# Value products of groups 16 to 19 in fp32 instead of six bf16 products each, with a new instruction order

## The chip, the cores and the metric

The kernel runs on one core of a Trainium2 chip. Its time is the device time of one execution in microseconds (us). The core has a matrix engine (TensorE, "PE" in the profile, with its weight loads as "PEld"), VectorE ("DVE"), ScalarE ("ACT"), GpSimd ("POOL"), and SyncE ("SP"), which here only issues the DMA transfers. Each engine works through its own queue in order.

## The reference, cut to what matters

Three layers follow one another. The first is a gated linear attention over 4 batches, 8 heads, 768 steps and 40 dimensions a head, the second a feed-forward layer that takes the largest of three products, and the third a feed-forward layer with a clipped activation.

```
for t in range(S):                       # S = 768, state C is 40x40 a head
    m_new  = max(f[t] + m, i[t])
    f_stab = exp(f[t] + m - m_new);  i_stab = exp(i[t] - m_new)
    C = f_stab*C + i_stab * outer(v[t], k[t])
    n = f_stab*n + i_stab * k[t]
    y[t] = sigmoid(o[t]) * (C @ q[t]) / max(abs(n . q[t]), 1)
x = y as 3072 tokens x 320
h = max(x @ w1, x @ w2, x @ w3)          # 320 -> 768
x = h @ w_out                            # 768 -> 320
h = x @ w_in                             # 320 -> 2048
out = (h * clip(h + 3, 0, 6) / 6) @ w_out2
```

## The kernel before, in words

The 768 steps are cut into six chunks of 128. A group `g` is one chunk of one batch with its 8 heads, so there are 24 groups; chunk `c` holds groups 4c to 4c+3. Within a group the recurrence becomes matrix products: `sc` (line 585) makes the scores of keys against queries, DVE multiplies them by the decay factors into the tile `fd` (line 601), and `pv` (line 663) multiplies that 128x128 tile of each head with the gated values `vt` (128 rows, 42 columns: 40 values and two for the denominator). `inter` adds what the state of the chunk before gives, `dc` makes the new state, `tr` transposes the finished group into `x1`.

The value product exists in two forms. For a group below `G3` it is one fp32 matmul a head. For the others, `vt` and `fd` are each split into three bf16 parts (functions `vr0`, `vr1` for the values and `pr0`, `pr1`, in two halves, for the scores: lines 648, 651, 657 and 661, six instructions a group on DVE or POOL), and the product is made of the six bf16 matmuls a head that `PARTS` lists:

```
pp = top(s["fd"]), top(s["pr"]), low(s["pr"])
vv = top(s["vt"]), top(s["vr"]), low(s["vr"])
for h in range(H):
    for n, (a, r) in enumerate(PARTS):
        nc.tensor.matmul(ps[:, h], pp[a][:, h], vv[r][:, h], start=n == 0, stop=n == len(PARTS) - 1)
```

The first feed-forward layer (`f_in`, line 325 for its products, and `f_out`, lines 913 and 915) runs on blocks of two or four groups as these get ready, in between the attention's matmuls. A first block needs groups 0 and 1. The second layer (`quad`, products at line 1251, output at line 1372) comes last, in 48 steps of a block of four groups and a pair of hidden slices. Its weights arrive as 64-bit numbers and are turned into two fp32r tiles each by ACT, DVE and POOL (`convert`, `pair_prep`, `o_prep`); the rows that are shared by four pairs are copied into each weight tile by DMA (`mix`, line 1138, three transfers a tile, 32 such copies in all).

Nothing decides the order at run time. `Plan` numbers all operations with what they depend on, the list `ORDER` says in which sequence they are issued (each engine takes its own operations out of that one list), the set `POOLS` says which of the operations that either may do go to POOL instead of DVE, and `JUNK` puts idle bf16 matmuls on a tile of ones (128x512, line 1444) ahead of some PE operations near the start, which fill gaps of PE there and give nothing to the result.

Of the kernel before, what the change touches and what calls it, by code (L numbers as in the profile page):

```python
# [29 lines left out]
NBC, GF, G3 = 4, 8, 16  # L30
# [10 lines left out]
1 990 2 4 5 6 991 992 7 8 993 10 11 9 13 14 994 900 20 918 902 901 19 995 12 40 903 904 919 15 18 16 23 905 920 50 22 21 921 922 17  # L41
24 42 906 907 923 39 912 28 908 914 62 930 913 44 41 43 25 27 63 45 26 909 46 910 47 911 29 915 916 105 924 64 917 48 49 51 960 65
30 31 67 66 931 37 84 932 936 32 33 61 926 925 52 106 53 54 942 927 68 34 38 72 3 35 36 55 59 108 107 111 81 82 94 928 60 56 933 86
69 57 58 85 89 929 110 71 70 109 112 128 948 934 1044 935 113 73 937 1045 938 943 944 939 74 1046 940 125 126 116 83 114 945 127
1048 75 88 941 950 122 1047 87 1052 117 946 947 129 115 1049 949 123 118 119 124 954 972 955 130 956 76 951 952 139 120 3290 1053
121 77 90 953 1054 996 957 140 141 1056 91 958 962 961 959 1055 1060 966 968 963 78 1050 93 92 964 967 965 103 95 133 151 969 984 79
1061 183 974 970 978 131 1057 80 973 1051 971 975 96 976 132 1062 1064 977 1063 97 104 135 979 980 981 1002 134 150 162 224 160 982
986 161 1008 98 99 1068 985 1065 137 136 983 138 164 100 101 998 1058 987 163 988 142 102 1059 1026 997 989 152 143 1069 153 999 144
1003 1000 1004 155 165 1001 1070 194 171 1066 166 172 1072 256 1076 1077 1067 1014 1071 167 1010 1009 1005 173 1073 182 1006 170
1011 145 146 1078 1012 1079 168 169 1007 1015 174 192 1016 196 1013 184 1080 1082 1017 195 1018 1086 1087 1020 1081 1083 203 193  # L50
1074 1021 1022 154 1023 1019 197 204 258 156 215 1088 1090 1027 1084 205 198 175 1085 226 176 1028 199 1024 1029 1025 225 1038 1075
1032 177 1089 1030 260 1091 1033 1034 200 1092 214 1096 1093 229 178 1097 1098 185 201 216 1031 228 235 206 236 237 157 202 1035 186
1039 1100 227 231 158 1036 1037 1099 1040 207 1041 1094 1042 1102 1101 1106 296 259 208 1103 147 1107 297 247 159 266 261 336 262
230 233 1104 1108 1110 232 263 264 234 218 268 1105 246 298 299 248 1109 300 257 265 238 1111 1095 188 338 301 148 267 1112 1113
1116 269 1117 1114 303 1118 1119 149 1120 304 187 239 376 1043 302 1122 1121 1123 1115 340 179 240 241 242 217 1126 1127 1128 1130
1134 1135 339 1129 219 270 272 287 306 271 189 1131 309 341 1136 1124 342 305 274 273 1138 220 1125 180 190 181 1141 1143 243 1137
307 276 277 1139 1142 327 343 1145 278 209 210 1149 1150 378 191 344 244 346 221 211 315 1132 245 1144 1146 222 1133 286 212 213 308
288 1151 1152 1153 1155 1159 316 275 279 1154 223 310 312 311 250 252 1160 1161 379 381 290 345 280 281 313 1156 1147 1148 1162 289
456 458 337 314 348 367 1163 1164 282 349 326 1165 318 380 317 1169 1170 352 1166 319 292 249 251 347 383 384 1171 1173 1157 253
1158 416 382 291 293 1172 350 354 459 418 1175 461 377 460 419 389 421 1179 1174 254 1176 283 1180 320 294 386 321 420 366 423 388  # L60
328 1167 1168 255 284 355 322 387 368 527 390 295 285 1181 1183 1182 1184 1185 1189 351 385 353 1190 356 323 1177 422 417 1186 357
1178 1140 1191 358 370 369 359 329 463 426 1193 1192 1194 464 392 1195 1196 396 1199 1200 1206 360 361 427 397 1204 536 424 462 1203
1187 1188 1208 1201 1207 428 394 391 1209 1202 538 539 496 362 371 1210 1214 331 393 425 398 1215 465 395 498 330 332 333 334 500
1197 466 335 399 1211 1198 499 406 429 324 325 1216 1217 501 540 431 432 407 400 497 1218 401 430 408 433 372 373 374 402 403 446
503 434 404 468 405 504 447 448 1219 1220 435 457 622 502 1224 1225 363 467 438 469 470 487 1212 364 365 471 436 541 1205 437 439
1213 1226 1227 473 509 440 472 486 506 1221 441 1228 442 375 488 1229 474 508 410 1230 1234 1235 576 443 409 444 412 476 515 507 475
510 1236 543 505 1231 544 542 578 1222 477 445 411 1223 413 1238 478 512 479 526 490 1237 1239 514 579 528 613 414 577 580 1240 624
1244 589 625 627 626 629 516 517 598 1245 511 1246 513 518 415 546 1232 581 1233 1241 547 548 545 583 519 449 489 586 584 582 1247
450 628 1248 1250 452 520 521 522 451 529 556 557 1249 1251 1254 1255 453 587 1242 1256 1258 1243 537 454 455 549 492 668 588 1257
1259 480 481 550 551 482 590 552 553 567 1260 1264 1265 670 1268 1252 630 585 714 491 493 554 566 523 558 555 530 568 1261 1253 559  # L70
560 671 1269 596 1271 1273 1266 1272 597 524 716 1267 599 494 717 673 672 675 719 1274 1275 591 593 1276 612 1279 525 592 632 631
1280 595 600 601 634 623 676 718 561 562 1262 1281 1283 563 1263 532 594 760 1282 1284 721 531 674 602 603 1285 533 483 1289 564
1270 565 604 495 1290 762 763 484 1286 669 681 690 614 485 1277 1278 570 572 722 569 605 642 638 1291 571 643 678 764 635 1292 1293
679 633 659 534 680 573 682 1294 636 1295 1299 1300 644 574 640 606 1287 641 677 535 765 683 685 1288 645 692 1296 767 1301 795 797
607 648 658 1302 1303 684 751 686 704 575 1304 694 660 1305 616 618 798 637 639 646 647 649 693 1306 1309 1310 1297 715 768 799 766
705 608 1311 695 688 1313 650 1298 727 1312 1314 720 723 1315 651 1319 1316 1320 1321 691 800 802 1307 652 653 1308 830 724 726 725
1322 1323 696 706 654 729 662 1324 728 687 832 615 769 689 833 617 1325 731 697 733 619 730 655 1326 732 620 770 698 750 761 699 700
1329 1330 796 1317 771 1318 801 778 734 740 1334 1331 736 1336 1337 1333 735 1332 1338 1340 1344 1345 752 1339 656 657 773 738 741
739 1341 737 661 663 772 1327 865 803 621 742 743 1328 701 744 834 781 664 707 804 782 609 702 1346 774 665 1347 1348 666 776 835
867 610 775 783 745 746 805 869 784 703 1350 836 777 785 786 837 831 838 667 1349 1354 747 1355 748 611 787 807 749 810 1351 1356  # L80
1342 1343 1357 812 806 1358 868 808 870 872 1360 1499 1500 840 813 708 1501 816 1502 814 1359 820 821 871 1503 1364 1365 779 1507
1352 1361 1353 815 841 843 809 811 780 1366 1368 788 1367 842 1505 1508 709 1504 1506 1370 1374 1375 789 866 1369 873 839 1376 818
1362 754 1363 819 817 1335 1510 1377 1371 874 1520 851 852 1512 1513 1521 1522 790 844 822 791 878 1378 710 711 1380 1384 1379 1385
1381 712 875 1372 1514 823 846 1373 886 877 845 792 1386 1387 1388 847 855 876 853 824 825 1390 1394 854 1515 756 753 713 755 757
758 856 880 879 1389 1395 881 1391 848 1401 888 1396 793 1382 882 1511 1523 1509 1524 1516 1527 1528 1397 1383 887 890 889 891 1402
1398 759 1525 1526 1403 857 849 850 858 826 1405 1399 892 884 859 1409 1529 1530 1404 1517 1518 860 861 885 1410 862 794 883 893 894
827 1519 895 896 1411 1531 1532 1406 1534 1536 1537 897 1547 828 1392 1393 1413 1573 863 1412 1533 829 898 864 1575 1414 1838 899
1415 1419 1574 1576 1577 1535 1544 1420 1421 1545 1546 1839 1407 1416 1408 1549 1840 1844 1538 1422 1550 1851 1539 1540 1551 1841
1842 1541 1423 1424 1425 1429 1430 1426 1553 1417 1552 1555 1554 1431 1418 1542 1585 1543 1843 1557 1847 1432 1556 1560 1570 1571
1433 1435 1434 1561 1567 1845 1586 1587 1558 1439 1436 1578 1579 1857 1588 1562 1580 1854 1581 1589 1582 1440 1609 1441 1563 1846  # L90
1427 1428 1591 1590 1611 1855 1592 1443 1583 1442 1610 1584 1848 1615 1616 1621 1860 1612 1444 1625 1593 1617 1445 1594 1596 1568
# [84 lines left out]
JUNK = {20: 17, 19: 5, 15: 2, 42: 1, 41: 2, 63: 6, 47: 1, 64: 4, 51: 3, 37: 1, 34: 1, 59: 1, 81: 2, 86: 1, 69: 1, 85: 2, 1044: 1, 116: 1, 139: 1, 120: 1, 95: 1, 1064: 1, 135: 2, 1070: 1, 171: 3}  # L176
# [1328 lines left out]
```

## Time and profile before

| | |
|---|---|
| median of 3 runs | 734.71 us (731.77 to 736.48) |
| profiled execution, its own time | 733.25 us |
| its span, first to last instruction | 731.5 us |
| PE busy in it | 721.8 us |
| DVE, ACT, POOL busy | 538.3, 386.1, 339.7 us |
| granted TensorE clock | 1.00 |

The span is what the hardware profiler recorded of the profiled execution; its time has 1.75 us more around it. Busy time is the time in which an engine had at least one instruction in work. Matmuls overlap each other, so that the duration of one is longer than the step from one start to the next; what a group of matmuls costs is read from the chain of work, where each piece has the time that it held up the next.

### The profile page before, as it was taken

The numbers are of one execution on the slowest core, as the hardware profiler recorded it, in microseconds if no ns is written. First come the engines' busy times: TensorE is split into PE (matmuls) and PEld (weight loads), VectorE is DVE, ScalarE is ACT, GpSimd is POOL, SyncE is SP. The second block draws the span as 40 slices with busy tenths as digits, with TensorE's granted clock in tenths as the row PEclk, the third lists the DMA queues.
The fourth block names the chain that finished last, engine by engine and source line by source line (L and its number), as shares of the span: only waits on it lengthen the run. The fifth ranks groups of instructions, "written<-read, shape, count | busy, mean of one in ns | idle before, by whom it ended". The sixth has DMA issues, their size and how long they took to land.

```text
span 731.5 us, 15227 instructions
## 1 busy us (share of the span) xinstructions
PE 721.8 (99%) x5685; PEld 654.9 (90%) x5685; DVE 538.3 (74%) x989; ACT 386.1 (53%) x867; POOL 339.7 (46%) x361
## 2 busy tenths in 40 slices
PE   9999999999999999999999999999999999999997
PEld 5789998888887788888888999999999999999997
DVE  6999987686877789687888788576566666567453
ACT  5776644234343244234777776545555555655543
POOL 3547664244345876773445372343433253443320
PEclk9999999999999999999999999999999999999999
DMA  8768675686676665724655521102100300300101
GB/s 268 250 210 291 194 240 187 191 239 212 199 228 198 191 202 180 227 76 143 217 181 178 162 79 59 37 1 59 37 2 1 95 1 1 95 1 1 37 2 37
DMA packets 57418, 95.22 MB, mean 130 GB/s; under 512 B 8096, under 2 KB 31872, under 8 KB 57344
## 3 DMA queue, kind: packets, MB, share of 16 engines
q1 hardware_dynamic: 57344, 94.24, 41.8%
q8 instruction: 45, 0.74, 0.4%
q14 instruction: 29, 0.24, 0.1%
HBM read 74.84 MB, written 17.65 MB: 126 GB/s over the span
## 4 chain that ended last, share of the span: by engine, by line
PE 89%; DVE 4%; DMA 3%; ACT 1%; issue 1%; POOL 1%; SPq 1%; ACTq 0%; DVEq 0%; POOLq 0%
PE h L325 25%; PE po L1372 22%; PE T L1251 12%; PE Q L1251 9%; PE acc L913 6%; PE pv L667 3%; PE sc L593 2%; PE acc L915 2%; PE pv L673 1%; PE dc L752 1%; DMA raw<-in_w 1%; PE tr L722 1%; PE in L625 1%; PE sc L597 1%; DMA kvo<-in_kvo 1%
## 5 line engine op out<-in xcount | busy, mean ns | idle before, releaser
L325 PE MATMUL h<-x,w 128*128 128x512 f32 (+1 forms) x1008 | 217.0, 366 | 0.0
L325 PEld LDWEIGHTS h<-x,w 128*128 128x128 f32 x1008 | 168.3, 189 | 27.8 <-ACT m L879 0.3
L1372 PE MATMUL po<-wo,gg 128*128 128x320 f32 x1152 | 192.5, 310 | 0.4 <-DVE gg L1328 0.4
L1372 PEld LDWEIGHTS po<-wo,gg 128*128 128x128 f32 x1152 | 172.3, 189 | 0.6 <-DVE gg L1328 0.6
L1328 POOL TENSOR_TENSOR gg<-cc,gg 128x512 fp32r<-128x512 f32 x48 | 63.2, 1319 | 141.2 <-ACT gg L1324 121.7
L1297 DVE TENSOR_TENSOR cc<-Q,s 128x512 f32<-128x512 f32 x96 | 53.1, 553 | 53.3 <-ACT s L1283 29.0
L1312 DVE SCALAR_TENSOR_TENSOR cc<-cc 128x512 f32<-128x512 f32 (+1 forms) x96 | 62.4, 654 | 36.0 <-ACT cc L1308 35.8
L1283 ACT COPY s<-T 128x256 f32<-128x256 f32 x144 | 52.8, 367 | 67.7 <-PE T L1251 50.8
L1324 ACT CAST gg<-cc 128x512 fp32r<-128x512 f32 x96 | 58.7, 621 | 33.9 <-DVE cc L1312 27.8
L1308 ACT ACTIVATE cc<-cc,b 128x512 f32<-128x512 f32 (+1 forms) x96 | 59.0, 617 | 27.4 <-DVE cc L1297 27.4
L913 PE MATMUL acc<-hh,w 128*128 128x512 f32 (+1 forms) x246 | 71.6, 370 | 0.0
L881 DVE TENSOR_TENSOR m<-h,m 128x512 f32<-128x512 f32 (+1 forms) x82 | 50.1, 611 | 20.4 <-PE h L325 17.8
L894 ACT CAST hh<-m 128x512 fp32r<-128x512 f32 (+1 forms) x41 | 23.0, 562 | 61.9 <-PE acc L913 60.8
L561 DVE TENSOR_TENSOR_SCAN fd<-fd,ident 128x512 f32<-128x512 f32 x40 | 52.3, 1315 | 2.5 <-DMA fd<-f_d 2.3
L913 PEld LDWEIGHTS acc<-hh,w 128*128 128x128 f32 x246 | 43.7, 188 | 6.9
L1328 DVE TENSOR_TENSOR gg<-cc,gg 128x512 fp32r<-128x512 f32 x48 | 36.7, 765 | 14.0 <-ACT gg L1324 13.9
L879 ACT COPY m<-h 128x512 f32<-128x512 f32 (+1 forms) x41 | 21.7, 528 | 42.3 <-PE h L325 31.3
L898 POOL TENSOR_TENSOR hh<-m,hh 128x512 fp32r<-128x512 f32 (+1 forms) x19 | 24.0, 1268 | 27.2 <-ACT hh L894 21.4
L601 DVE TENSOR_TENSOR fd<-sc,fd 128x512 f32<-128x512 f32 x48 | 32.0, 681 | 4.8 <-PE sc L593 2.5
L667 PEld LDWEIGHTS pv<-vt,fd 128*128 128x128 f32 x256 | 30.4, 192 | 0.8
L667 PE MATMUL pv<-vt,fd 128*128 128x42 f32 x256 | 30.4, 280 | 0.0
L915 PE MATMUL acc<-hh,w 128*128 128x512 f32 (+1 forms) x82 | 29.3, 364 | 0.0
(338 smaller groups left out, 1410.9 us busy)
## 6 DMA issues: line engine op xcount, KB each, us to landing
kvo<-in_kvo SPq DMA_DIRECT2D x22, 488.0 KB
fd<-f_d SPq DMA_DIRECT2D x20, 512.0 KB
qs_d<-q SPq DMA_DIRECT2D x48, 160.0 KB
raw<-in_w SPq DMA_DIRECT2D x18, 384.0 KB
qs<-qs_d SPq DMA_DIRECT2D x80, 80.0 KB
qraw<-in_qkf SPq DMA_DIRECT2D x16, 320.0 KB
qs<-qs_d SPq DMA_DIRECT2D x32, 160.0 KB
rawo<-in_w2o SPq DMA_DIRECT2D x16, 320.0 KB
```

What stands on the lines that cost most here:

```text
L325: nc.tensor.matmul(ps, wt[:, a:a + 128], x[:, r], start=n == 0, stop=n == len(order) - 1)
L561: nc.vector.tensor_tensor_scan(out=half, data0=s.get(("bc", a), half), data1=ident4.rearrange("p h t -> p (h t)"), initial=0.0, op0=ALU.mu ...
L667: nc.tensor.matmul(ps[:, h], s["fd"][:, h], s["vt"][:, h], start=True, stop=True)
L913: nc.tensor.matmul(acc[a], wo[:, a * 128:128 + a * 128], h, start=first, stop=last)
L1251: nc.tensor.matmul(ps, w[0:rows, a], x[0:rows, b], start=start and n == 0, stop=n == 3, skip_group_check=not start)
L1283: nc.scalar.copy(s["s", two][:, i % 2], s["T"])
L1297: nc.vector.tensor_tensor(out=x, in0=y, in1=s["s", i == 0], op=ALU.add)
L1308: nc.scalar.activation(s["r"][:, a:b], src, AF.Relu, bias=b3)
L1312: nc.vector.scalar_tensor_tensor(out=s["cc"][:, a:b], in0=s["r"][:, a:b], scalar=6.0, in1=src, op0=ALU.min, op1=ALU.mult)
L1324: nc.scalar.copy(GG[j, p][:, 0, a:b], s["cc"][:, a:b])
L1328: eng.tensor_tensor(out=g[:, 1, a:b], in0=s["cc"][:, a:b], in1=g[:, 0, a:b].bitcast(F32), op=ALU.subtract)
L1372: nc.tensor.matmul(po[j, t], x, WO[2 * p + e][:, o:o + OC], start=first and z == 0, stop=last and z == 2)
```

## The change: four groups' value products and a new order

`G3` goes from 16 to 20. So groups 16 to 19 take the fp32 form of `pv`, and their 24 splitting instructions are gone. As the operations are numbered anew, `ORDER`, `POOLS` and `JUNK` are all replaced.

```diff
-NBC, GF, G3 = 4, 8, 16
+NBC, GF, G3 = 4, 8, 20
...
-JUNK = {20: 17, 19: 5, 15: 2, 42: 1, 41: 2, 63: 6, 47: 1, 64: 4, 51: 3, 37: 1, 34: 1, 59: 1, 81: 2, 86: 1, 69: 1, 85: 2, 1044: 1, 116: 1, 139: 1, 120: 1, 95: 1, 1064: 1, 135: 2, 1070: 1, 171: 3}
+JUNK = {20: 16, 19: 1, 15: 4, 41: 4, 63: 3, 29: 3, 51: 4, 37: 1, 34: 2, 56: 2, 120: 2, 116: 2, 122: 1, 114: 1, 1028: 1, 139: 1, 1038: 1, 150: 1, 100: 3, 171: 2}
```

The lists `ORDER` and `POOLS` are too long to show (3291 numbers before, 3267 after). Taking one engine's operations out of each list and matching them by what they write gives this:

| read from the two lists | before | after |
|---|---|---|
| PE, ACT, SP operations | 881, 847, 288 | 881, 847, 288 |
| DVE, POOL operations | 930, 340 | 934, 312 |
| operations of free choice that change engine | | 130 POOL to DVE, 119 DVE to POOL |
| idle matmuls ahead of the first product of layer one | 51 | 40 |
| idle matmuls behind it | 11 | 15 |
| DVE: place of the scan over gates of chunks 1 to 5 (line 370) | 26th, between `y` of group 0 and the reciprocals of group 1 | 18th, ahead of the scores of group 1 |
| SP: place of the load of those gates | 13th | 8th, ahead of the weights (0,1), (0,2) and (1,1), the q and k of group 1, and the k, v and o of group 2 |
| `mix` copies with at most one PE operation between issue and reader | 5 of 32 | 0 of 32 |
| `mix` copies with at most five | 9 of 32 | 1 of 32 |

The sequence of PE's operations is nearly the same in both: the `pv` of groups 16 to 19 stand at places 214, 236, 242 and 256 before and at 207, 226, 238 and 253 after, and the transposes that end the attention at 310 and 309 or 310.

## Rows read from the trace of the kernel before

**Rows 1.** Head of the page: busy us (share of the span) and instructions.
```profile
PE 721.8 (99%) x5685; PEld 654.9 (90%) x5685; DVE 538.3 (74%) x989; ACT 386.1 (53%) x867; POOL 339.7 (46%) x361
```

**Rows 2.** Busy time by stretch of the span; columns as its second line says.
```profile
core 0: us, PE busy (x) PEld busy (x) DVE busy (x) ACT busy (x) POOL busy (x), PEclk, DMA share, GB/s
0.00:30.64 30.64, 28.85 (x220) 18.05 (x221) 24.37 (x49) 19.23 (x40) 14.86 (x26) 1.00 0.83 252
30.64:221.00 190.36, 189.97 (x1655) 166.53 (x1655) 157.11 (x297) 90.71 (x206) 92.64 (x105) 1.00 0.72 223
221.00:333.00 112.00, 111.62 (x1058) 91.10 (x1057) 89.14 (x149) 38.23 (x83) 79.80 (x82) 1.00 0.57 173
...
381.00:421.00 40.00, 37.57 (x245) 34.54 (x244) 32.30 (x63) 30.23 (x78) 19.24 (x25) 1.00 0.55 167
```

**Rows 3.** All waits of PE, eight lines: us in total, times, longest.
```profile
PE wps L1444 <- DVE gm L366: 1.5, 1, 1.5
PE T L1251 <- DMA w_4d<-mix_d1d: 1.2, 1, 1.2
PE T L1251 <- ACT s L1283: 1.2, 1, 1.2
...
PE tr L722 <- DVE x L733: 0.2, 1, 0.2
```

**Rows 4.** Chain of work, one group's value product: start us, us, what.
```profile
76.62 1.91 PE pv L667 x16
...
207.57 1.72 PE pv L667 x16
226.23 1.22 PE pv L673 x48
...
305.95 1.20 PE pv L673 x48
```

**Rows 5.** Weight loads of the two forms (lines 667, 673): ns min/median/max.
```profile
L667 PEld LDWEIGHTS pv<-vt,fd x256: 186/192/201, 16.9 to 209.0; 128*128 128x128 f32 x128
...
L673 PEld LDWEIGHTS <-fd x192: 96/97/103, 226.1 to 330.0; 128*128 128x128 bf16 x192
```

**Rows 6.** Sum over all stretches for the split tiles, `pr` and `vr`.
```profile
sum 731.60, PE 10.28 PEld 9.42 DVE 5.70 POOL 31.36; mean PE 1.71 PEld 1.57 DVE 0.95 POOL 5.23
...
sum 731.60, PE 10.49 DVE 4.31 POOL 8.36; mean PE 1.75 DVE 0.72 POOL 1.39
```

**Rows 7.** Chain of work up to the first product of layer one.
```profile
7.32 8.10 DMA raw<-in_w
...
16.48 1.24 issue
...
22.47 0.15 DVE gm L369
...
22.64 1.54 DVE gm L370
...
26.97 0.22 PE wps L1444
...
30.64 0.48 PE h L325 x4
```

**Rows 8.** Idle matmuls (line 1444) ahead of and behind that product.
```profile
0.00:30.64 30.64, 16.07 (x51) 4.99 (x51) 1.00 0.83 252
30.64:221.00 190.36, 3.77 (x11) 0.99 (x11) 1.00 0.72 223
```

**Rows 9.** Issues on SP's queue: the raw weights (0,1) and the second gates.
```profile
5.15 0.36 SPq L284 DMA_DIRECT2D raw<-in_w  x1
...
10.84 0.33 SPq L361 DMA_DIRECT2D gf<-in_fg  x1
12.00 0.33 SPq L362 DMA_DIRECT2D gi<-in_ig  x1
```

**Rows 10.** Chain of work where the second layer begins: transfers and SP's queue.
```profile
383.75 3.08 DMA rawo<-in_w2o
387.40 2.88 DMA raw<-in_w2m
...
414.31 2.20 SPq L1138
417.95 1.41 DMA w_4d<-mix_d1d
```

258 rows, old and new, of tables (ORDER, POOLS) are left out of this document.

## The prediction

> **What bounds the kernel now.** I began with the head of the page: PE is busy for 721.8 of 731.5 us [rows 1]. A busy matrix engine could still be one that stretches its work, so I went on to the table by stretch. From the first product of layer one at 30.64 us until 381 us PE is idle for well under a microsecond in a hundred, and the clock is 1.00 throughout [rows 2]. DVE comes next, at 157 of 190 us and then 89 of 112; it is close, but it isn't the bound. Third, PE's own list of waits. It has eight lines. Leave out the 1.5 us at the very start, and the other seven, from 1.2 down to 0.2, add up to 4.4 us [rows 3]; 2.4 of them lie between 381 and 421 us, where the second layer begins (40.00 less 37.57) [rows 2]. So behind 30.64 us the time is the sum of PE's work plus 4.4 us. Ahead of it the chain does not run on PE: it is a weight transfer of 8.10 us, then DVE, and PE fills the time with idle matmuls [rows 7, 8]. This gives the rule for every edit: work added to PE behind 30.64 us costs its full length, work taken off DVE or POOL is worth at most the waits that it ends, and ahead of 30.64 us only the DMA and DVE chain counts.
>
> **The value products.** In the chain of work the 16 matmul records of a group in fp32 hold 1.72 us, once 1.91, and the 48 records of a group in bf16 hold 1.22 or 1.20 [rows 4]. They are fewer, but each step is longer: 1.72 / 16 = 108 ns against 1.22 / 48 = 25 ns. The weight loads show why the fp32 form does not profit from its smaller count: one takes 192 ns against 97 [rows 5], and with 42 columns behind each load the products are too short to cover it. Per group the change costs PE 1.72 - 1.22 = 0.50 us, for four groups +2.0 us, all of it on the path. The far end is the dearest fp32 row against the cheapest bf16 row, 1.91 - 1.20 = 0.71, which makes 2.8. I take 2.0, since 1.7 is what stands beside full-length matmuls as here.
>
> Here a rule speaks the other way. The Trainium skill, "FP8 and Floating Point Precision", section "TensorE Precision Notes", says that a true fp32 product takes four passes through the array. With bf16 passes of 25 ns that would be, as an estimate from this page, 8 x 4 = 32 passes or 0.8 us a group, 0.4 less than the 48 of bf16, and the sum would hold -1.7 instead of +2.0. The fp32 groups of this trace contradict it at this shape, with 1.72 us measured; it is kept below as a rival with a small chance.
>
> **The splitting work that goes.** Over all eight split groups `pr` holds DVE for 5.70 and POOL for 31.36 us, `vr` 4.31 and 8.36 [rows 6]. Half of that, 24 instructions, is 24.9 us, some 20 of it on POOL. None of it lies on the chain while PE is full, so directly it is worth 0. What it can be worth indirectly is limited by the 4.4 us of PE waits, of which hardly any falls where these groups run (0.38 us of idle time in 221 to 333 us). I enter 0. The cover is PE's own backlog; if PE were not full there, DVE's share would come onto the path.
>
> **The start.** In the old order DVE's scan over the later gates, with the small copy ahead of it 1.54 + 0.15 us, stands on the chain between group 0's output and group 1's reciprocals, and group 1 is the last thing that the first block waits for [rows 7]. The new order puts it eight places earlier, near the point where the chain shows 1.24 us in which DVE has nothing released [rows 7]. So about 1.5 us of it leaves the chain. Late next is the weight transfer. The load of these gates also moves, on SP's queue, from 10.84 us to about where the raw weights (0,1) were issued at 5.15 [rows 9], ahead of three weight transfers, q and k of group 1 and the load of group 2. It is 2 x 32 x 640 x 4 bytes = 164 KB, 0.6 us at the 252 GB/s of this stretch [rows 2], and it delays all five. The scan also gets a new place to wait: if its gates are late, the scores of group 1 queue behind it on DVE, and PE's `pv` of group 1 behind those. The start therefore gains between 11 x 0.22 = 2.4 us (the eleven idle matmuls fewer, each 0.22 on the chain [rows 7]) and loses up to 0.6. I take -1.5, the row of the scan itself.
>
> **Idle matmuls behind the start.** There are 15 now; the old order had 11 [rows 8]. PE is full there, so four more cost 4 x 0.22 = +0.9 us, or nothing if they stand where PE waits anyway.
>
> **Where the second layer begins.** Two of PE's waits of 1.2 us are here, one of them for a `mix` copy into a weight tile [rows 3], which was held up 2.20 us in SP's queue before its transfer of 1.41 [rows 10]. The new list issues these copies with a longer lead: only one of 32, instead of nine, has five PE operations or fewer ahead of its reader. I count that wait as gone, -1.2. What is late next is the conversion chain (raw transfers of 3.08 and 2.88 us [rows 10], then ACT, DVE, POOL), which I leave as it is. The ends: -2.4 if all idle time in the stretch goes, and +7.1 if the cover of the chain is lost (below).
>
> **Engines swapped.** 130 operations go from POOL to DVE and 119 the other way; DVE gets four operations more in all, POOL 28 fewer. With DVE at 83% [rows 2] this is nearly balanced, and I enter 0. It is the term that I know least: it can open a wait of a microsecond or two anywhere.
>
> **Sum.** 733.25 + 2.0 + 0.9 - 1.5 - 1.2 = 733.4 us, against the profiled execution. That execution was 1.5 us below the median of the three runs (734.71), so on the scale of the median I forecast 734.9 us: no change that can be seen.
>
> **The rivals.**
> - *Slower: the start of the second layer loses its cover.* Between 381 and 421 us four links of transfer and queue, 3.08 + 2.88 + 2.20 + 1.41 = 9.6 us, lie on the chain, while PE loses only 2.4 us [rows 2, 10]; ACT, DVE and PE are all above 75% there. If the new order brings the first weight tiles late, PE, which takes its products in order, pays the remaining 7.1 us: 734.9 + 1.2 + 7.1 = 743.2 us. It begins to decide once these tiles are more than about 7 us later against PE's work than now. For it: conversions there move by several us both ways in the lists. Against: the copies, which caused the largest wait, get more lead.
> - *Faster: the relief closes the waits.* With 25 us less splitting work all 4.4 us of PE's waits go and the start gains its full 2.4: 733.25 + 2.0 + 0.9 - 4.4 - 2.4 = 729.4, or 730.8 against the median. For it: DVE at 83%. Against: the waits lie elsewhere than the relief. Even this is within 1%, because PE has no more idle time to give.
> - *The fp32 products are cheap.* If a group cost PE 0.4 us less instead of 0.5 more, the sum is 3.7 us lower, 731.2. Against: sixteen groups in this trace at 1.7 to 1.9 us [rows 4].
>
> **How the numbers follow.** The forecast gets 0.75, the slower rival 0.08, the relief 0.11, cheap fp32 products 0.03, and 0.03 stays for a gain that no row shows. One per cent, 7.3 us, is about what a measurement can tell from no change. Forecast, relief and cheap products all lie within it, so "within 1%" has 0.75 + 0.11 + 0.03 less 0.02 for a relief that also shortens PE's work, 0.87; faster has 0.05, slower 0.08. The range goes from 729.5, the relief less a microsecond for the spread of the runs, to 741.0: the dear ends of products (+0.8) and start (+2.1), the wait not ended (+1.2), and 2 us for a new wait.
>
> **What would show it.** In the profile after: 320 fp32 records of `pv` and 192 bf16 ones, with 1.7 us for each of the four new groups in the chain. First product of layer one at about 29 us, without the long scan ahead of it. No PE wait for a `mix` copy. PE idle for 3 to 4 us behind the start. I am wrong if PE's waits between 381 and 421 us grow past 6 us, if DVE passes 95% in a stretch and PE waits for it, or if the fp32 groups take under 1.2 us.

## The result, and the profile after

| | before | after |
|---|---|---|
| median of 7 runs each, one chip | 733.28 us (731.77 to 736.48) | 743.19 us (738.86 to 751.96) |
| ratio, 95% interval | | 1.0125 [1.0093, 1.0157] |
| profiled execution | 733.25 us | 751.96 us |
| its span, mean granted clock | 731.5 us, 1.00 | 750.2 us, 0.984 |

The kernel is slower by 1.25%, some 9 us, and outside the forecast range. The profiled execution of after is the slowest of its seven, 1.8% above the fastest of them, and is one of two that the ratio leaves out. In after the names stand two lines higher than in before: `pv` at 665 and 671, `h` at 323, the idle matmuls at 1442.

The head of the page, with the granted clock in 40 slices, answers to [rows 1]:

```profile
PE 736.2 (98%) x5550; PEld 665.5 (89%) x5550; DVE 538.4 (72%) x994; ACT 384.4 (51%) x867; POOL 308.1 (41%) x335
...
PEclk9589999999999999999999999999999999999999
```

PE is busy 14.4 us longer although it has 135 instructions fewer, and the second and third slice of the clock row read 5 and 8. POOL lost 31.6 us of work, more than the some 20 of the splitting, and the time did not follow it. The same stretches as [rows 2], with the same columns:

```profile
0.00:30.64 30.64, 27.49 (x131) 17.84 (x133) 17.42 (x34) 12.62 (x26) 11.24 (x21) 0.79 0.76 224
30.64:221.00 190.36, 186.35 (x1615) 161.91 (x1611) 155.36 (x288) 89.43 (x205) 89.06 (x100) 0.97 0.68 209
221.00:333.00 112.00, 110.88 (x849) 91.15 (x848) 82.38 (x149) 38.77 (x82) 47.39 (x53) 1.00 0.64 188
381.00:421.00 40.00, 40.00 (x205) 33.96 (x204) 30.12 (x63) 31.39 (x82) 20.03 (x28) 1.00 0.59 172
```

Two places are worse. From 30.64 to 221 us PE is idle for 4.0 us (0.39 before), and the mean clock of the first two stretches is 0.79 and 0.97. One is better: at 381 to 421 us, where PE had lost 2.4 us, it loses nothing. (The same microseconds are not the same work there: the last product of layer one starts at 403.7 us, before at 383.6. But from 381 to 441 us PE has no idle time either.) Cut at the points where the clock changes, the start reads so:

```profile
0.00:17.76 17.76, 14.61 (x73) 7.42 (x75) 12.24 (x25) 9.13 (x18) 6.82 (x15) 1.00 0.89 248
17.76:34.83 17.07, 17.07 (x111) 13.65 (x108) 7.56 (x16) 5.92 (x14) 6.12 (x8) 0.50 0.52 167
34.83:45.07 10.24, 9.07 (x78) 7.26 (x76) 9.95 (x17) 7.82 (x17) 4.85 (x6) 1.00 0.64 179
45.07:51.89 6.82, 6.82 (x35) 5.28 (x31) 4.35 (x11) 4.58 (x15) 3.53 (x6) 0.50 0.69 212
```

TensorE ran at half clock, 1.2 instead of 2.4 GHz, for 17.07 + 6.82 us; half of that, 11.9 us, is what it cost, as an estimate. PE's idle time grew from 9.7 to 14.0 us (span less busy), and four products at the price forecast are 2.0 us: 11.9 + 4.3 + 2.0 = 18.2 of the 18.7 us between the two spans. PE's own list of waits (us in total, times, longest) answers to [rows 3]:

```profile
PE dc L750 <- issue: 2.4, 1, 2.4
PE wps L1442 <- DVE gm L364: 1.5, 1, 1.5
PE h L323 <- ACT m L877: 1.3, 2, 1.1
PE sc L595 <- DMA qs<-in_qk: 1.2, 2, 0.8
PE tr L720 <- POOL y L711: 0.8, 1, 0.8
```

The mix copy is gone from it. In its place stand a state product `dc`, hidden-layer products `h`, and the scores `sc` of group 1; the list of before has no wait above 0.4 us ahead of the second layer but the 1.5 us at the very start.

The chain of work at the start (start us, us, what) shows the last of these; the three `pv` rows at its end answer to [rows 4]:

```profile
3.10 5.35 DMA qs<-in_qk
8.46 8.81 DMA qs<-in_qk
17.41 1.74 PE sc L595 x14
19.15 1.40 PE wps L1442 x3
20.55 3.27 PE pv L665 x16
...
37.67 1.12 DVE t L303
...
272.27 1.91 PE pv L665 x16
289.09 1.80 PE pv L665 x16
306.70 1.22 PE pv L671 x48
```

The scores of group 1 are released by the transfer of its q and k, which took 8.81 us of the chain; right behind, the clock is half and a value product takes 3.27 us. The queue of SP shows that it was issued later; the last line is that transfer in the kernel before:

```profile
4.77 0.42 SPq L359 DMA_DIRECT2D gf<-in_fg  x1
5.24 0.42 SPq L360 DMA_DIRECT2D gi<-in_ig  x1
6.53 0.35 SPq L282 DMA_DIRECT2D raw<-in_w  x1
8.05 0.79 SPq L471 DMA_DIRECT2D qs<-in_qk  x2
```
```profile
5.55 1.18 SPq L473 DMA_DIRECT2D qs<-in_qk  x2
```

With the gates loaded first, the raw weights follow at 6.53 us (5.15 before [rows 9]) and the q and k of group 1 at 8.05, 2.5 us later than before. The first product of layer one starts at 37.75 us, not at the 29 that was forecast.

### The profile page after: what moved, and what is told of

Its sections match the earlier page's. It is cut to its first block, busy times and chain, and to the rows that moved or that the text cites. A ratio compares the mean times of both kernels' runs of the same rounds, so it can differ in the third digit from the quotient of the medians.

```text
span 750.2 us, 14934 instructions
## 1 busy us (share of the span) xinstructions
PE 736.2 (98%) x5550; PEld 665.5 (89%) x5550; DVE 538.4 (72%) x994; ACT 384.4 (51%) x867; POOL 308.1 (41%) x335
## 4 chain that ended last, share of the span: by engine, by line
PE 85%; DVE 6%; DMA 4%; issue 2%; ACT 1%; SPq 1%; POOL 0%; ACTq 0%; DVEq 0%; POOLq 0%
PE h L323 23%; PE po L1370 21%; PE T L1249 12%; PE Q L1249 9%; PE acc L911 6%; PE pv L665 4%; DMA qraw<-in_qkf 2%; DMA qs<-in_qk 2%; PE acc L913 2%; PE sc L591 2%; PE dc L750 2%; PE wps L1442 1%; PE tr L720 1%; PE sc L595 1%; DVE cc L1310 1%
## 5 line engine op out<-in xcount | busy, mean ns | idle before, releaser
L323 PE MATMUL h<-x,w 128*128 128x512 f32 (+1 forms) x1008 | 222.1, 369 | 1.5 <-ACT m L877 1.3
L1326 POOL TENSOR_TENSOR gg<-cc,gg 128x512 fp32r<-128x512 f32 x41 | 53.9, 1318 | 126.6 <-ACT gg L1322 108.4
L1310 DVE SCALAR_TENSOR_TENSOR cc<-cc 128x512 f32<-128x512 f32 (+1 forms) x96 | 65.5, 686 | 27.9 <-ACT cc L1306 27.6
L911 PE MATMUL acc<-hh,w 128*128 128x512 f32 (+1 forms) x246 | 71.2, 370 | 0.0
L1326 DVE TENSOR_TENSOR gg<-cc,gg 128x512 fp32r<-128x512 f32 x55 | 44.1, 806 | 13.3 <-ACT gg L1322 13.2
L665 PEld LDWEIGHTS pv<-vt,fd 128*128 128x128 f32 x320 | 41.3, 206 | 1.8 <-issue 1.1
L665 PE MATMUL pv<-vt,fd 128*128 128x42 f32 x320 | 41.3, 293 | 0.3 <-issue 0.3
L896 POOL TENSOR_TENSOR hh<-m,hh 128x512 fp32r<-128x512 f32 (+1 forms) x17 | 19.7, 1159 | 50.5 <-ACT hh L892 49.0
L1207 POOL TENSOR_TENSOR xr<-xr 128x512 f32<-128x512 f32 x18 | 24.6, 1366 | 18.6 <-DMA out<-x2o 9.8
```

Of the source, the lines that this page charges most:

```text
L323: nc.tensor.matmul(ps, wt[:, a:a + 128], x[:, r], start=n == 0, stop=n == len(order) - 1)
L665: nc.tensor.matmul(ps[:, h], s["fd"][:, h], s["vt"][:, h], start=True, stop=True)
L911: nc.tensor.matmul(acc[a], wo[:, a * 128:128 + a * 128], h, start=first, stop=last)
L1310: nc.vector.scalar_tensor_tensor(out=s["cc"][:, a:b], in0=s["r"][:, a:b], scalar=6.0, in1=src, op0=ALU.min, op1=ALU.mult)
L1326: eng.tensor_tensor(out=g[:, 1, a:b], in0=s["cc"][:, a:b], in1=g[:, 0, a:b].bitcast(F32), op=ALU.subtract)
```

## The experiments

The theory that I formed from this: three things lose the time, the granted clock at the start, new waits of PE between 50 and 350 us, and the fp32 products. The rivals: the products alone; the early load of the gates alone; the idle matmuls alone. All were timed over five rounds beside the kernel before; a ratio below is to that kernel.

"Without the clock" below is an estimate: of each execution's time its span times one less its mean granted clock is taken off, and the median of a kernel's executions stands. It gives 732.1 us for the kernel before (97 executions) and 738.5 for after. So of the 9.9 us between the medians 6.4 are the order and the products, and some 3.5 the clock. The 6.4 fit the trace: 4.3 us more idle time of PE and 2.0 us for the products.

**The products alone: old order, twenty groups.** The old lists with the 24 splitting operations dropped and the rest renumbered.

```diff
-NBC, GF, G3 = 4, 8, 16
+NBC, GF, G3 = 4, 8, 20
```

> The old order with only the products of groups 16 to 19 in fp32 and their 24 splitting instructions left out; idle matmuls as before. Product theory (the four fp32 groups are dear): 740 us or more, like the changed kernel. Start theory (the loss comes from the first 50 us of the new order): 735.3 us, the 2.0 us that the chain of the kernel before gives for the products, at a granted clock of 1.00. Middle theory (waits that the new order opens between 80 and 380 us): 735.3 us as well; this run parts it from the product theory only.

735.45 us, ratio 1.0008 [0.9983, 1.0033]. The four groups in its chain of work, and then PE where the second layer begins:

```profile
226.30 1.73 PE pv L666 x16
251.93 1.71 PE pv L666 x16
261.05 1.71 PE pv L666 x16
276.38 1.72 PE pv L666 x16
287.53 1.22 PE pv L672 x48
```
```profile
221.00:333.00 112.00, 111.80 (x921) 92.37 (x920) 82.13 (x139) 38.48 (x83) 61.65 (x66) 1.00 0.53 171
381.00:421.00 40.00, 39.00 (x252) 35.87 (x251) 33.84 (x66) 31.37 (x82) 21.12 (x26) 1.00 0.61 185
```

6.87 us for the four, less 4 x 1.22: 2.0 us, the price that I had entered. Behind them PE stands 1.7 us later than in the kernel before (the 700th product of layer one at 279.54 us against 277.80), but between 381 and 421 us it idles 1.00 us instead of 2.43, and by 462 us it is only 0.1 us behind. It seems that the later arrival gave the late mix copy the time that PE had waited for it: that wait is gone from PE's list. But this is one execution, at 733.36 us among the fastest of the twelve. Over all twelve the estimate without the clock is 734.7, 2.6 us above the kernel before, so that the products come back is not shown for most executions. Between nothing and 2.6 us is the products' share of the slowdown; the rest is the order.

**The start, four parts of it.** First the load of the gates alone, moved ahead of the weights (0,1) on SP in the old kernel (operation 105):

```diff
-24 42 906 907 923 39 912 28 908 914 62 930 913 44 41 43 25 27 63 45 26 909 46 910 47 911 29 915 916 105 924 64 917 48 49 51 960 65
+24 42 105 906 907 923 39 912 28 908 914 62 930 913 44 41 43 25 27 63 45 26 909 46 910 47 911 29 915 916 924 64 917 48 49 51 960 65
```

> The old kernel with one SP entry moved: the load of the gates of chunks 1 to 5 stands ahead of the weights (0,1), as in the new order. Start theory: the q and k of group 1 land later, PE waits for them near 16 us, the clock is granted at half for some stretch behind that, and the time goes to 736 to 745 us. Product and middle theories: 733 to 734 us, the transfer is hidden.

735.25 us, ratio 1.0022 [0.9985, 1.0058], without the clock 732.1: level with before, under the 736 of the start theory. 9 of its 12 executions had a clock below 0.999, of the kernel before 40 of 97 (10 of 24 timed beside it), too few to part the two. Its profile has the new kernel's wait, and the clock behind it:

```profile
PE sc L597 <- DMA qs<-in_qk: 0.7, 1, 0.7
```
```profile
0.00:18.42 18.42, 16.18 (x94) 9.10 (x94) 11.39 (x24) 10.02 (x21) 6.90 (x15) 1.00 0.87 268
18.42:32.07 13.65, 13.65 (x77) 10.12 (x76) 8.57 (x17) 4.62 (x11) 5.62 (x8) 0.50 0.62 199
```

Then the reverse in the new kernel: the load behind the weights (1,1), the scan ahead of the reciprocals of group 1 (operations 105 and 106; all lines between are wrapped anew).

```diff
-966 968 1 2 4 5 6 967 7 8 10 894 969 11 970 971 13 876 878 12 17 877 14 879 895 880 40 18 896 881 9 20 22 897 19 15 16 898 45 105 23
-50 21 882 24 42 39 44 41 888 43 906 899 28 900 84 25 26 27 62 46 884 883 890 889 63 106 47 29 891 885 892 49 48 886 893 887 30 31 32
...
+966 968 1 2 4 5 6 967 7 8 10 894 969 11 970 971 13 876 878 12 17 877 14 879 895 880 40 18 896 881 9 20 22 897 19 15 16 898 45 23 50
+21 882 24 42 39 44 41 888 43 906 105 899 28 900 84 25 26 27 62 46 884 883 890 889 63 47 29 891 885 892 49 48 886 893 887 30 31 32
+33 64 51 901 52 61 902 67 907 37 38 34 65 66 106 53 59 54 68 35 81 930 83 903 904 85 94 36 60 55 56 107 108 111 905 3 82 908 57 58
...
```

> The new kernel with the load of the gates behind the weights (1,1) on SP, and the scan over them back ahead of the reciprocals of group 1 on DVE, as in the old order. Start theory: no wait of PE for q and k of group 1, clock 0.999 or more, 735 to 737 us. Middle theory: 740 us or more still. Product theory: 740 us or more still.

741.91 us, ratio 1.0096 [1.0059, 1.0132], and 738.2 without the clock, as after. The wait for q and k is gone from its list, but the clock falls later, at 36.11 to 42.93 us, behind PE waits for ACT, DVE and POOL of 0.4 to 0.9 us. The start theory's 735 to 737 us was missed: the early load isn't the main loss. That it makes the early fall isn't shown either, since a run below has the wait and the fall with the old start.

A third kernel moved one more step: the cast of the weights (1,2) on ACT (operation 916) further back.

```diff
-69 72 109 86 1020 1022 909 918 912 924 129 70 71 914 112 113 110 913 910 911 73 1021 120 124 915 916 87 125 128 116 1023 74 920 936
+69 72 109 86 1020 1022 909 918 912 924 129 70 71 914 112 113 110 913 910 911 73 1021 120 124 915 87 125 128 116 1023 74 920 936 121
```

> The new order with late gates (as e3), and one ACT operation moved: the cast of the weights (1,2), which waits for a join on DVE, stands behind the eviction of group 2's products and of the first gate transpose instead of ahead of them. Start theory: PE no longer waits for ACT there near 35 us, the two waits of 0.6 us go, the clock stays up, 736 to 738 us. Middle theory: 740 us or more, as in e3.

741.81 us, ratio 1.0089 [1.0057, 1.0122]: no different from the run before it, and the forecast of 736 to 738 us missed. One execution of six, at clock 1.0, took 736.53 us; the others 740.0 to 744.1. This stays unclear.

**The idle matmuls.** The new numbers of `JUNK` in the old kernel, 55 for 62, and the old ones in the new kernel; and seven more in the new kernel ahead of the scores of group 1.

```diff
-JUNK = {20: 17, 19: 5, 15: 2, 42: 1, 41: 2, 63: 6, 47: 1, 64: 4, 51: 3, 37: 1, 34: 1, 59: 1, 81: 2, 86: 1, 69: 1, 85: 2, 1044: 1, 116: 1, 139: 1, 120: 1, 95: 1, 1064: 1, 135: 2, 1070: 1, 171: 3}
+JUNK = {20: 16, 19: 1, 15: 4, 41: 4, 63: 3, 29: 3, 51: 4, 37: 1, 34: 2, 56: 2, 120: 2, 116: 2, 122: 1, 114: 1, 1052: 1, 139: 1, 1062: 1, 150: 1, 100: 3, 171: 2}
```

> The old kernel with the idle matmuls of the new one (55 instead of 62, ahead of the same operations as in the new order). Clock theory (the number and place of idle matmuls keeps the clock up at the start): clock below 0.997 in most runs and 736 to 742 us. Start theory without this (late weights and waits, not the idle matmuls): 733 to 734 us, clock as in the kernel before.

738.14 us, ratio 1.0051 [1.0027, 1.0075]: slower, with every other operation where it was. Without the clock it is 732.1, the time of before; 11 of 12 executions had a clock below 0.999. In its profile PE idles 3.5 us ahead of the fall (1.5 of it at the very start, as in before):

```profile
0.00:33.80 33.80, 30.27 (x238) 20.96 (x239) 27.14 (x56) 22.41 (x47) 16.30 (x26) 1.00 0.85 260
33.80:40.63 6.83, 6.83 (x29) 4.35 (x28) 4.88 (x11) 2.45 (x8) 2.73 (x4) 0.50 0.69 222
```

In the new kernel the old numbers, each ahead of the operation that it stood ahead of:

```diff
-JUNK = {20: 16, 19: 1, 15: 4, 41: 4, 63: 3, 29: 3, 51: 4, 37: 1, 34: 2, 56: 2, 120: 2, 116: 2, 122: 1, 114: 1, 1028: 1, 139: 1, 1038: 1, 150: 1, 100: 3, 171: 2}
+JUNK = {20: 17, 19: 5, 15: 2, 42: 1, 41: 2, 63: 6, 47: 1, 64: 4, 51: 3, 37: 1, 34: 1, 59: 1, 81: 2, 86: 1, 69: 1, 85: 2, 1020: 1, 116: 1, 139: 1, 120: 1, 95: 1, 1040: 1, 135: 2, 1046: 1, 171: 3}
```

> The new kernel, with the idle matmuls of the kernel before (62, each number ahead of the operation that it stood ahead of there) in place of its own 55. Theory (the new order's idle matmuls let the granted clock fall early; they are part of the loss): 738.5 to 740.5 us, granted clock above 0.995 in most executions. Rival (the clock falls for the order's own waits, whatever the idle matmuls): 742 to 744 us, clock as in the new kernel.

744.68 us, ratio 1.014 [1.0096, 1.0183], 738.5 without the clock: the theory missed and the rival held. And seven more:

```diff
-JUNK = {20: 16, 19: 1, 15: 4, 41: 4, 63: 3, 29: 3, 51: 4, 37: 1, 34: 2, 56: 2, 120: 2, 116: 2, 122: 1, 114: 1, 1028: 1, 139: 1, 1038: 1, 150: 1, 100: 3, 171: 2}
+JUNK = {20: 16, 19: 1, 15: 4, 41: 4, 63: 3, 29: 3, 51: 4, 37: 1, 34: 2, 56: 2, 120: 2, 116: 2, 122: 1, 114: 1, 1028: 1, 139: 1, 1038: 1, 150: 1, 100: 3, 171: 2, 47: 7}
```

> The new kernel with seven more idle matmuls ahead of the scores of group 1, where PE waits for their q and k. The wait itself stays, only the clock can change. Start theory in its form that the clock carries most of the loss: clock 0.998 or more, 735 to 738 us, with a smaller spread than 739 to 752. If the late transfer itself is the loss: 740 us or more at the same clock. Middle theory: 740 us or more.

744.97 us, ratio 1.0134 [1.0089, 1.0178]: nothing gained. Without the clock it is 741.7, 3.2 us more than the new kernel: the seven delay what stands behind them. The wait for q and k is gone from PE's list, but its profile has half clock from 39.55 to 42.96 us behind waits of 1.4 and 0.6 us for DVE and ACT. So neither number of idle matmuls, 55 or 62, is good or bad by itself: the new ones let the clock fall in the old order, and the old ones don't keep it up in the new.

**Where the order loses.** Hybrids: every engine follows the old order, with its idle matmuls, up to a certain operation of PE, and the new order from there; all have twenty groups in fp32. To the 50th operation, about 50 us (against the new kernel, the list's first line):

```diff
-966 968 1 2 4 5 6 967 7 8 10 894 969 11 970 971 13 876 878 12 17 877 14 879 895 880 40 18 896 881 9 20 22 897 19 15 16 898 45 105 23
+1 966 2 4 5 6 967 968 7 8 969 10 11 9 13 14 970 876 20 894 878 877 19 971 12 40 879 880 895 15 18 16 23 881 896 50 22 21 897 898 17
```

> Hybrid: the old lists up to PE's 50th operation (about 49 us), idle matmuls included, the new lists for all that is left; products of groups 16 to 19 in fp32. Start theory (the loss arises while PE waits behind ACT and DVE near 35 us, with the drop of the clock there): 735 to 736 us, clock 0.999 or more. Middle theory (waits of the new order between 50 and 380 us): 737.5 us or more at a clock of 0.998 or more.

To the 214th, about 221 us (against that hybrid, the first line that differs):

```diff
-144 979 976 980 155 165 977 1046 194 171 1042 166 172 1048 256 1052 1053 1043 990 1047 215 986 981 173 985 987 170 167 996 154 988
+144 979 976 980 155 165 977 1046 194 171 1042 166 172 1048 256 1052 1053 1043 990 1047 167 986 985 981 173 1049 182 982 170 987 145
```

> Hybrid: the old lists up to PE's 214th operation (about 224 us), the new ones behind that; products of groups 16 to 19 in fp32. Start theory: 734 to 736 us, as with e5. Middle theory, if the loss lies between 50 and 220 us: 734 to 736 us here, 737.5 or more in e5. If the new order loses behind 221 us: 737 us or more here as well.

To 50 us: 741.84 us, ratio 1.0088 [1.0062, 1.0115], without the clock 739.4. To 221 us: 737.06 us, ratio 1.0054 [1.0029, 1.008], without the clock 736.3. So the order between 50 and 221 us costs about 3 us (739.4 less 736.3), and behind 221 us about 1.6 (736.3 less the 734.7 of the old order with twenty groups). By the same estimate the start costs nothing but its clock (739.4 with the old start, 738.5 with the new, six and seven executions). The first one's waits behind the start, and what DVE, POOL and PE did at the longest (start us, us, what; in brackets the idle time before it):

```profile
PE h L323 <- ACT m L877: 2.6, 4, 1.5
PE dc L750 <- issue: 2.4, 1, 2.4
```
```profile
97.61 0.51 DVE L571 TENSOR_TENSOR vt<-kvo,idt 128x336 f32<-128x336 f32 x1 [0.91 <-DMA kvo<-in_kvo]
98.16 0.42 DVE L879 TENSOR_TENSOR m<-h,m 128x256 f32<-128x256 f32 x1
98.50 1.04 DVE L711 TENSOR_TENSOR y<-nm,sg 128x320 f32<-128x320 f32 x1
99.46 1.70 DVE L578 TENSOR_TENSOR vw<-vt,fd 128x336 f32<-128x336 f32 x1
99.27 1.52 POOL L507 TENSOR_TENSOR q<-qraw,q 128x640 bf16<-128x640 f32 x1
101.26 1.09 PE L750 MATMUL dc<-vw,kvo 128*64 128x42 f32 x16 [2.35 <-issue]
```

The list names "issue" for `dc`, but it starts at 101.26 us, right where DVE's `vw`, its operand, ends (99.46 + 1.70). DVE had first waited 0.91 us for the load of k, v and o, then done `m` and `y`. And `y` and `vw` were slow: 1.04 and 1.70 us, while POOL worked on `q` from 99.27 us. In the trace of after DVE has 29 such instructions (`vt`, `vw`, `y`, all 128 rows in f32). The 18 with no POOL instruction beside them took 0.48 to 0.51 us, the 11 with one 0.53 to 1.69; in the kernel before 18 of 19 took at most 0.51. No run changes this alone, but it makes up to 1.8 of the 2.4 us, and the sums of DVE and POOL don't show it. During the wait, from 100.77 us, the clock falls to half, until 111.01 us. The same wait of 2.35 us in after, up to 114.55 us, has no half clock behind it.

**Two waits mended.** In the hybrid to 50 us: that load one place up on SP (257), `vw` ahead of `y` on DVE (270, 242), and at 158 us the maximum's copy ahead of a cast on ACT that waits for a load (1183, its lines left out here):

```diff
-239 315 262 1094 1096 300 376 1095 1090 1098 303 265 1091 407 302 304 1097 1099 179 257 1102 338 340 1018 240 1019 180 306 1103 213
-1104 1106 305 339 1105 181 378 271 241 187 1110 1111 1117 269 1107 341 242 270 1100 342 380 189 272 1112 1114 190 1101 343 191 273
+239 315 262 1094 1096 300 376 1095 1090 1098 303 265 257 1091 407 302 304 1097 1099 179 1102 338 340 1018 240 1019 180 306 1103 213
+1104 1106 305 339 1105 181 378 271 241 187 1110 1111 1117 269 1107 341 270 242 1100 342 380 189 272 1112 1114 190 1101 343 191 273
...
```

> The run with the old order to 50 us and the new one behind it (741.84 us, clock 0.993 in its profile), with the two longest TensorE waits of 50 to 221 us taken away by three moves: the load of the ninth group's keys and values one place up on SP and its weighted values ahead of the normalised rows on VectorE (the wait of 2.4 us at 98.7 us), and one maximum's first copy ahead of a cast that waits for a load on ScalarE (1.5 us at 158 us). Theory (these waits are the loss between 50 and 221 us): 737.5 to 739 us, and no fall of the granted clock near 101 us. Rival (the waits only move on to the next late step): 741 to 742 us.

738.07 us, as the theory had it; ratio 1.0075 [1.0044, 1.0105], without the clock 737.1, 2.3 us less than its twin. Its five executions at a clock of 0.999 or more took 736.4 to 738.0 us, the one such of the twin 739.55. The intervals of the two ratios overlap; what supports it is the place. The stretch ahead of this `dc` in the twin, and then `vw`, `dc` and the stretch around them in this kernel. Its profiled execution reaches the place some 7 us later, because its clock was half from 15 to 35 us, but that lateness doesn't close the wait: after reaches it 13 us later than the twin and waits the same 2.35 us.

```profile
96.00:101.20 5.20, 2.90 (x33) 2.69 (x30) 4.24 (x8) 3.57 (x8) 2.67 (x3) 0.96 0.89 271
```
```profile
107.43 0.50 DVE L578 TENSOR_TENSOR vw<-vt,fd 128x336 f32<-128x336 f32 x1
108.64 0.67 PE L750 MATMUL dc<-vw,kvo 128*64 128x42 f32 x16
101.20:111.00 9.80, 9.80 (x101) 9.36 (x100) 8.22 (x21) 5.83 (x14) 4.81 (x7) 1.00 0.86 265
```

So three moves among 3267 operations give back some 2 of the 3 us: these waits are a large part of the loss there. The moves were not parted: the load, the order on DVE and the absence of POOL work beside `vw` came together. And the second wait only moved on: the one at 158 us is gone, but PE waits 1.1 us for the same copy at 183 us. The half clock from 15 to 35 us stood behind a wait of 0.9 us for q and k of group 1 at 12.3 us, in a start that is the old one. So that wait comes without the early load too.

**The tail.** The old order to PE's 334th operation, about 350 us, the new one behind it, with twenty groups and with the sixteen of the kernel before (the first line that differs from the old order, with twenty):

```diff
-1580 1596 1583 1589 1598 1376 1621 1427 1600 1603 1428 1663 1627 1576 1623 1622 1429 1431 1435 1436 1624 1604 1625 1626 1590 1605
+1580 1596 1583 1589 1598 1376 1621 1427 1600 1603 1428 1663 1627 1576 1623 1622 1429 1431 1435 1834 1825 1826 1590 1605 1628 1604
```

> Twenty groups in full precision; every engine follows the old order up to TensorE's 334th operation (about 350 us, behind the last attention product), the new order from there. Theory (the new order loses its time ahead of 350 us, and gains some behind it, since the old order's TensorE waits of 1.4, 1.4 and 0.5 us near 390, 418 and 448 us are not in the new one): 732 to 734.5 us, 0.5 to 2.5 us under the all-old order with the same products (735.45), about level with the kernel before. Rival (the order behind 350 us is one of the places where the new order loses): 737 us or more.

> The kernel before with its sixteen groups in full precision; every engine follows the old order up to TensorE's 334th operation (about 350 us), the new order from there. Theory (the tail of the new order is worth what the old one's waits near 390, 418 and 448 us cost): 730 to 732 us, 1.5 to 3 us under the kernel before, faster than both kernels. Rival (those waits hide behind something else that ends last): within 1 us of the kernel before; rival that the new tail loses time: 736 us or more.

737.38 us, ratio 1.0066 [1.0038, 1.0095], and 734.82 us, ratio 1.0011 [0.9986, 1.0036]. Neither beats the kernel before, and both theories missed: a wait of 1.8 us for ACT, which neither order has, opened at the seam.

```profile
PE h L325 <- ACT m L879: 1.8, 1, 1.8
```

So both again, with that step put ahead of five others on ACT (operation 1467, and 1466 of PE with it; here with sixteen groups):

```diff
-1630 1632 1642 1653 1693 1634 1454 1859 1643 1633 1605 1460 1635 1636 1639 1694 1601 1657 1464 1456 1631 1447 1463 1461 1658 1659
-1448 1462 1466 1468 1660 1467 1661 1641 1662 1665 1566 1654 1663 1470 1655 1474 1469 1648 1649 1569 1650 1471 1475 1664 1688 1602
+1630 1632 1642 1653 1693 1634 1454 1859 1643 1633 1605 1460 1635 1636 1639 1694 1601 1657 1464 1456 1631 1447 1466 1467 1463 1461
+1658 1659 1448 1462 1468 1660 1661 1641 1662 1665 1566 1654 1663 1470 1655 1474 1469 1648 1649 1569 1650 1471 1475 1664 1688 1602
```

> The run with the kernel before to 350 us and the new order behind it (734.82 us), with one ScalarE step of the fifth block's next product (a maximum's first copy) put ahead of five others, so that the TensorE wait of 1.9 us at 374 us, made by the seam between the two orders, closes. Theory (the new order's tail is worth the three waits near 390, 418 and 448 us that it lacks, and loses some 1.5 us of it again behind 536 us): 732 to 733.5 us, level with or a little under the kernel before. Rival (the tail brings nothing, whatever the seam): 734.5 to 735.5 us.

> The run with twenty groups in full precision, the old order to 350 us and the new one behind it (737.38 us), with the same ScalarE step put ahead. Theory: 733 to 735.5 us, 1.5 to 2 us above its twin with sixteen groups, since the new tail has not the waits in which the old one gave the 1.7 us of the products back. Rival (the products cost nothing here either): level with the twin.

Sixteen groups: 734.98 us, ratio 1.0014 [0.9986, 1.0042]. Twenty: 736.36 us, ratio 1.0031 [1.0006, 1.0055]. The wait shrank to 1.2 us, a miss of my edit, and with it the tail is worth nothing to the kernel before, as the rival had it: in the trace of the run with sixteen groups PE is 1.0 us behind the kernel before at 351 us, 0.9 ahead at 535 us, when the waits at 381 to 421 us are passed, and 0.8 behind again at 720 us. The twins differ by 1.9 us without the clock (733.3 and 735.2): with a tail in which the old waits of the second layer are gone, the four products cost what they take.

## Why the prediction was wrong, point by point

| kernel, all with twenty groups | ratio to before | without the clock, us (before: 732.1) |
|---|---|---|
| old order throughout | 1.0008 [0.9983, 1.0033] | 734.7 |
| new order behind 350 us, seam wait shortened | 1.0031 [1.0006, 1.0055] | 735.2 |
| new order behind 221 us | 1.0054 [1.0029, 1.008] | 736.3 |
| new order behind 50 us | 1.0088 [1.0062, 1.0115] | 739.4 |
| new order throughout | 1.0125 [1.0093, 1.0157] | 738.5 |

Each step of the ratio is about as wide as its interval, so none stands by itself but the sum does. (With the seam's wait as it was, the second row reads 1.0066.) Without the clock the largest step, 3.1 us, is the order from 50 to 221 us; behind 221 us it is 1.6 us, some of which may be waits of the seams. The start has no step but in the ratio, which holds the clock.

- **Engines swapped, entered at 0: the first step that failed.** I had written that it "can open a wait of a microsecond or two anywhere", and gave that 2 us at the end of the range. It opened several, and PE's idle time grew by 4.3 us in place of 0: in after 2.4 us at `dc`, 1.1 at `h` and 0.8 at `tr`; in the hybrid to 50 us 1.5 at `h`, at 158 us; in the hybrid to 221 us 1.2 at `h` for ACT, 0.9 at `tr`, 0.8 at `h` for DVE. With PE idle for 0.39 us in 190 [rows 2], a new order of the others could only lose there. The balance of the sums on DVE and POOL said nothing on this: neither on the distance between a producer and its PE reader, nor on the time that an instruction of DVE takes beside one of POOL. And the term was about engines alone; the order of the operations on SP, ACT and DVE behind the start had none, and the longest wait came in part from there.
- **The start, entered at -1.5: the second.** "The eleven idle matmuls fewer, each 0.22" were a gain only while the clock stayed at 1.00, which the sum took for granted: the clock had no term. Their new numbers alone cost 0.51% in the old order, by the estimate all of it clock. While the clock held, the first product did come earlier: at 28.40 us in the new order with late gates, at 29.66 with seven more idle matmuls, against 30.29 before. The early load was bounded at 0.6 us by its bytes; in the new order its q and k were issued 2.5 us later, in the old order with the early load 1.6 us (7.18 against 5.55). In that one it is worth 0 in time without the clock, with a PE wait of 0.7 us for q and k in its profile (1.2 in after). The point "if its gates are late" was the wrong way round: the gates came early and the q and k late.
- **The products, +2.0:** right, 1.99 us in the chain, 1.9 between the twins. In the profiled execution of the old order 1.6 us of it came back at the waits of the second layer, which I hadn't coupled to it; over its executions that isn't shown (2.6 us without the clock). The rival that counts four bf16 passes by the Trainium skill, "FP8 and Floating Point Precision", "TensorE Precision Notes", gets no support: 6.87 us for four groups, where it had 0.8 us a group. (108 ns is the step of a record; with two records a head a product takes 215 ns.)
- **The splitting work, 0:** right. In the old order with twenty groups POOL lost 19.2 us and DVE 6.4, and the kernel was no faster.
- **The mix copies, -1.2:** right at their place; PE's idle time there is 0. But the tail as a whole gains nothing (734.98 us with sixteen groups).
- **Idle matmuls behind the start, +0.9:** not measured by itself; all the new numbers together left the old order at 732.1 without the clock, as before.
- **The slower rival** (743.2 us) had the right number at the wrong place: the second layer's start lost no cover at all, and none of PE's waits behind 381 us is above 0.4 us. Its chance of 0.08 was for another mechanism and does not count as foresight.

What stays open: what decides in a given execution whether the clock falls. The hybrid to 221 us, whose first rows are those of the kernel before, had it fall at 18.33 us with no PE wait ahead but the 1.5 us at the very start. And which of the small waits take back, behind 535 us, what the new tail gains at 381 to 421 us.

## What to carry to other kernels

When an engine is full, a new order written for a small change has little gain to find (here 2.4 us of waits) and many waits to open: keep the old order and change the one thing. The engines' sums don't price a reordering. The distance from each operand's producer to its reader on the full engine is where these waits lay, but whether it would have forecast them was not tried. Idle matmuls that fill gaps belong to one order and are costed by the clock, not by their length. Work added to a full engine may be given back at the next place where it waits for something that comes on its own time, as one profile showed.

## What the runs showed of the hardware

The granted clock fell to half (1.2 instead of 2.4 GHz) for 3.4 to 23.9 us at a time, mostly in the first 50 us, and it differed between executions of one kernel: from 0.981 to 0.998 on the mean for after. The profiles in which PE waited for a q and k transfer of group 1 for 0.7 us or more (after, the early load, the two mended waits, the old idle matmuls in the new order) all have half clock next (from 17.76, 18.42, 15 and 21 us). But such a wait is neither enough nor needed elsewhere: the wait of 2.4 us at `dc` has half clock with it in the hybrid to 50 us and none in after, waits of 1.8 us at the seam near 375 us and of 1.2 and 1.2 us near 390 and 418 us in the kernel before [rows 3] have none, and the hybrid to 221 us falls without one. Where it fell, it cost up to 11.9 us (half of 23.9, an estimate), so a step that is worth 0 in time can cost half a per cent by the clock alone, as the idle matmuls did.

An instruction of DVE that takes 0.5 us alone took up to 1.7 us while POOL had one in work (29 instructions in the trace of after).
